# Attention with scaled-and-summed value blocks: halving the pieces of a finished tile's end, and where they are put

## The chip, the cores and the metric

The kernel runs on one core of one Trainium2 chip. The metric is the device time of one launch in microseconds (us): lower is better. Before the change three runs took 559.68, 562.78 and 559.63 us, median 559.68 us.

## What is computed

```python
xn = layernorm(x)                                  # x: 2048 x 448
q  = (xn @ wq) in 16 heads of 256                  # 8 key/value heads, each for two query heads
p  = softmax(q @ k.T / 16)                         # the last 512 cached keys
s  = concat(p @ v) @ wo                            # 2048 x 448
g  = silu((gelu(xn @ w_gate) * (xn @ w_up)) @ w_down)
out = x + s * g
```

The kernel multiplies each value head by its rows of `wo` once, before the attention, so that `p @ (v @ wo)` is added straight into the output sums of a tile, over all 16 heads.

## The kernel before, in words

The first 165 us or so compute the layernorm, the feed-forward part (its gate is written to DRAM) and the products of values and `wo` (`vw`). The rest, which the change touches, is a loop over `NST` = 128 steps (L1045 on): 8 chunks (`c`) of 256 rows times 16 heads (`h`). A chunk is two output tiles of 128 rows. Step n does four things, each in program order on its engine:

- TensorE (PE) makes the scores of step n (`s_jobs`, from `kT` and `qT`, into a ring of three PSUM banks 4 to 6), the queries of step n+2 (`q_jobs`, bank 7), and the product of probabilities and `vw` of step m = n-4 (`pv_jobs`). Every matmul uses 64 of the 128 rows of the array; `halves` (L796) takes two lists, one for the lower and one for the upper 64 rows, and lays them out in one order so that the two halves run side by side. Two matmuls of different halves that add into the same PSUM bank must not overlap: where the half changes on a bank, `halves` makes the second one wait for the end of the first.
- VectorE (DVE) takes a reciprocal of the row sums of step n-1 (`rd`, L863), the row minima of the step's two score tiles (`mn`, L852), and four sums of blocks of the transposed probabilities (`sS`, L888, called `sums`) of step n-3, which PE reads in step n+1.
- ScalarE (ACT) empties the queries (`qT`, L378) and takes the two exponentials (`p`, L857), each of which frees a score bank.
- GpSimd (POOL) multiplies by the reciprocal (the normalizing, `pn`, L873, two tiles a step); a DMA issued by SP then transposes it into `pT`.

The product uses seven block products instead of eight, a fast matrix multiplication over 2 x 2 blocks: products 1 to 7, of which 5, 6, 7 and 3 read `sS`. They are added over the 16 heads in banks 0 to 3 (`AT`, L891): bank 0 holds products 1 and 2, bank 1 products 6 and 7, bank 2 products 4 and 5, bank 3 product 3. `B0` to `B3` are the lists of matmuls of each bank, 4, 4, 4 and 2. `pv_plan` (L915) gives the order in which a head's lists are issued: `one` and `two` to one half, `all_` to the other.

When head 15 of a chunk has been added (a step with `ends`, n = 19, 35, 51, ..., 115), banks 0 to 3 must be emptied into `aS` (seven blocks of 128 x 224, f32) before the next chunk's first head may write them: `evac` (L941), bank 0 and bank 1 by DVE, 2 and 3 by ACT. `finish` (L949) then returns nine pieces that add up the blocks on POOL, multiply by the gate on DVE (`fin`, L964, 128 x 448) and add x on POOL (`add`, L974, 128 x 448); one piece is popped per step (L1106), at the end of the step's program, and the result is stored by a DMA on SP. Each POOL piece has `after=last_sum`: it waits for the last of DVE's four sums of that step. POOL works in order, so the normalizing of the next step stands behind it.

After step 127 a tail adds up the last chunk.

Of the kernel before, what the change touches and what calls it, by code (L numbers as in the profile page):

```python
# [6 lines left out]
ALU = mybir.AluOpType  # L7
# [159 lines left out]
def bass_recurrent_scan__sliding_block_cached__geglu_ffn__prompt_kernel(  # L167
# [36 lines left out]
    with es:  # L204
# [14 lines left out]
        def sbuf_bufs(at, size, n):  # L219
            return [K.buf(at + i * size, size) for i in range(n)]  # L220
# [66 lines left out]
        aS, a, at = place("aS", [P, 7, HN], F32, at=tl)  # L287
        b_aS = sbuf_bufs(a, HN * 4, 7)
        tmp, a, at = place("tmp", [P, 2, D], F32, at=at)
        b_tmp = sbuf_bufs(a, D * 4, 2)  # L290
        NXR = 4
        ofin, a, at = place("ofin", [P, 2, D], BF16, at=at)
        b_ofin = sbuf_bufs(a, D * 2, 2)
        xr, a, at = place("xr", [P, NXR, D], BF16, at=at)
        b_xr = sbuf_bufs(a, D * 2, NXR)
        gr, a, at = place("gr", [P, NXR, D], BF16, at=at)
# [74 lines left out]
        def dma(q, o, i, reads=(), writes=()):  # L371
            K.op(q, lambda e, o=o, i=i: e.dma_start(o, i), reads, writes, dma=True)
# [4 lines left out]
        def act(o, i, func, reads, writes, scale=1.0):  # L377
            K.op("act", lambda e, o=o, i=i: e.activation(o, i, func, scale=scale), reads, writes)  # L378
# [525 lines left out]
        def pv_jobs(n, u, lst, last):  # L904
            h, src = n % Hq, pv_src(n)
            rows = slice(R * u, R * u + R)
            out = []
            for p, j in lst:
                i, s = AT[p]
                a, b = src[p]  # L910
                out.append([i, s * HN, (s + 1) * HN, a[rows, j, :], vw[rows, vslot(h), p - 1, j, :],
                            h == 0 and (u, (p, j)) in FIRST, (u, (p, j)) in last, [b, b_vw[h][p - 1]]])
            return out

        def pv_plan(n):  # L915
            if n % Hq in (0, Hq - 1):
                one, two, all_ = B0 + B2, B3 + B1, B0 + B1 + B2 + B3
            else:
                one, two, all_ = B0 + B2, B1 + B3, B1 + B3 + B2 + B0
            last = LAST if n % Hq == Hq - 1 else TLAST if n == NST - LAG - 1 else ()  # L920
            u = 0 if n + LAG + 2 < NST else 1
            return pv_jobs(n, u, one, last), pv_jobs(n, u, two, last), pv_jobs(n, 1 - u, all_, last)

        def flat(x):
            return [z for y in x for z in y]
# [8 lines left out]
            moves.append(lambda: dma("sp", gr[:, t % NXR, :], gd[t, :, :], (b_gd[t],), (b_gr[t % NXR],)))  # L934

        def store_out(t):
            moves.append(lambda: dma("sp", out_view[:, t, :], ofin[:, t % 2, :], (b_ofin[t % 2],), ()))
            if t + NXR < NT:
                load_fin(t + NXR)

        def evac(i, eng):  # L941
            n = 2 if i < 3 else 1
            o, s = aS[:, 2 * i:2 * i + n, :], bank[i][:, 0:n * HN].rearrange("p (a n) -> p a n", a=n)
            if eng == "act":
                act(o, s, ACT.Copy, (b_ps[i],), b_aS[2 * i:2 * i + n])
            else:
                K.op("dve", lambda e: e.tensor_copy(o, s), (b_ps[i],), b_aS[2 * i:2 * i + n])

        def finish(c, eng):  # L949
            def tt(o, a, b):  # L950
                def go():
                    sl = [aS[:, x[0]:x[-1] + 1, :] for x in (o, a, b)]
                    if len(a) < len(o):
                        sl[1] = sl[1].broadcast_to([P, len(o), HN])
                    K.op(eng, lambda e: e.tensor_tensor(sl[0], sl[1], sl[2], ALU.add),  # L955
                         [b_aS[i] for i in a + b], [b_aS[i] for i in o], after=last_sum)
                return go

            def fin(x):
                def go():  # L960
                    t = 2 * c + x
                    s, y = t % 2, t % NXR
                    sl = slice(1, 7, 5) if x == 0 else slice(4, 6)
                    K.op("dve", lambda e: e.scalar_tensor_tensor(  # L964
                        out=tmp[:, s, :].rearrange("p (a n) -> p a n", a=2), in0=aS[:, sl, :], scalar=sc[:, 1:2],
                        in1=gr[:, y, :].rearrange("p (a n) -> p a n", a=2), op0=ALU.mult, op1=ALU.mult),
                        [b_aS[i] for i in range(7)[sl]] + [b_sc, b_gr[y]], (b_tmp[s],))
                return go

            def add(x):  # L970
                def go():
                    t = 2 * c + x
                    s, y = t % 2, t % NXR
                    K.op(eng, lambda e: e.tensor_tensor(ofin[:, s, :], tmp[:, s, :], xr[:, y, :], ALU.add),  # L974
                         (b_tmp[s], b_xr[y]), (b_ofin[s],), after=last_sum)
                    stores.append(t)
                return go
            return [(eng, tt([1, 2], [0], [1, 2])), (eng, tt([3], [2], [3])), (eng, tt([0], [2], [5])),
                    (eng, tt([4, 5], [3], [4, 5])), ("dve", fin(1)), (eng, add(1)), (eng, tt([6], [0], [6])),
                    ("dve", fin(0)), (eng, add(0))]  # L980


        heads = [*range(3, 13), 2, 13]
        order = []
# [57 lines left out]
            K.reuse(b_gsl[t:t + 1])  # L1042
            act(gsl[:, t, :], gr[:, y, :], ACT.Copy, (b_gr[y], b_sc), (b_gsl[t],), scale=sc[:, 1:2])

        todo, stores, ready, last_sum = [], [], [], []  # L1045
        fill(0)
        for n in range(NST):
            h, m = n % Hq, n - LAG
            c = n // Hq
            more = n + 2 < NST  # L1050
            ends = m >= 0 and m % Hq == Hq - 1
            if n == LAG:
                store_g()
                K.reuse(b_pT[3:] + b_sS[2])
            s0, s1 = s_jobs(n, 0, True), s_jobs(n, 1, not more)
            for t in ready:
                store_out(t)
            ready, stores = stores, []
            if moves and n < NST - 2:
                moves.pop(0)()  # L1060
            if more:
                q0, q1 = q_jobs(n + 2, 0), q_jobs(n + 2, 1)
                q0[1][0][5] = True
                (q1[0] if m >= 0 else q1[1])[-1][6] = True
                if m < 0:
                    q1[0][0][5] = q0[0][-1][6] = True
            if m < 0:
                halves(q1[0] + s0[0] + q0[0] + s1[0], q0[1] + s1[1] + q1[1] + s0[1])
            else:
                one, two, all_ = pv_plan(m)  # L1070
                if more:
                    halves(s0[0] + one + q0[0] + q1[0] + s1[0] + two, q0[1] + q1[1] + s0[1] + s1[1] + all_)
                else:
                    halves(s0[0] + s1[0] + all_, one + s0[1] + s1[1] + two)
            if n >= 1:
                recip(n - 1)
                norm(n - 1)
            row_min(n, 0)
            if more:
                q_evac(n + 2)  # L1080
            if ends:
                evac(0, "dve")
                evac(2, "act")
            row_min(n, 1)
            expo(n, 0)
            expo(n, 1)
            if 3 <= n < NST - 1:
                last_sum = [sums(n - 3, (0, 1, 2, 3))]
            if n < 3:
                fill(n + 1)  # L1090
            if n == 2:
                store_g()
            if n in VW12:
                vw_plain(VW12[n])
            if n in GS:
                gates_scaled(GS[n])
            if n == LAG:
                K.reuse(b_aS + b_tmp + b_ofin + b_xr + b_gr)
                for t in range(NXR):
                    load_fin(t)  # L1100
            if ends:
                evac(1, "dve")
                evac(3, "act")
                todo.extend(finish(m // Hq, "pool"))
            elif todo:
                todo.pop(0)[1]()  # L1106
            if h == LAG and c >= 1 and c + 1 < NC:
                for k in range(NK + 1):
                    moves.append(lambda k=k, y=(c + 1) % 2, d=xnd[c + 1, :, k, :], r=b_xnd[2 * c + 2:2 * c + 4]: dma(
                        "sp", xq[:, y, k, :], d, r, (b_xq[y][k],)))  # L1110
# [57 lines left out]
        for t in range(2):  # L1168
            i, sl = PB[t], (slice(1, 7, 5), slice(4, 6))[t]
            p = two(p32[:, t, 0:D])  # L1170
            add("dve", p, two(bank[i][:, 0:D]), gs[t], [b_ps[i], b_gsl[t]], (b_p32[t],), ALU.mult)
            add(("pool", "dve")[t], two(ofin[:, t, :]), p, aS[:, sl, :], [b_p32[t]] + [b_aS[k] for k in ((1, 6), (4, 5))[t]],
                (b_ofin[t],))
            store_out(NT - 2 + t)
            moves.pop(0)()

# [54 lines left out]
```

## Time and profile before

| what | value |
|---|---|
| median of the three runs | 559.68 us |
| profiled execution: its time / its span | 560.88 us / 559.1 us |
| granted TensorE clock (mean) | 0.999 |
| evacuation, DVE 128 x 448 f32 (L947) | 0.621 us each, 12 after 260 us |
| POOL add of blocks, 128 x 448 / 128 x 224 (L955) | 1.134 / 0.658 us |
| POOL add of x, 128 x 448 (L974) | 1.041 us |
| DVE multiply by the gate, 128 x 448 (L964) | 0.678 us |
| DVE add, one input in PSUM, 128 x 224 (tail, L1114) | 0.380 us |
| POOL normalizing, 128 x 512 (L873) | 0.713 us, two per step |
| DVE sums, 128 x 256 f16 (L888) | 0.282 us median, 0.693 and 0.764 at most |
| matmul of the products, 64 rows x 224 columns | 0.256 us each, several in flight |

The busy time of an engine is the union of its instructions; a matmul's duration includes the time in the pipeline, so two or more overlap. The start of the reciprocal L863 marks the step on DVE; the start of the matmuls with `wqr` marks it on PE.

### The profile page before, as it was taken

To read this page: it belongs to the slowest core of one execution; us is meant where nothing else is said; L and a number is where in the kernel's file an instruction comes from. 1 tells how busy PE (TensorE), PEld (TensorE's weight loads), DVE (VectorE), ACT (ScalarE), POOL (GpSimd) and SP (SyncE) were. 2 spreads that over 40 slices of the span, in tenths; PEclk is the share of its full clock that TensorE was granted. 3 is DMA by queue.
4 is the path that set the end of the run, shared out by engine and by line. 5 is a ranking of instruction groups with operands and counts; after the bars stand their busy time and mean duration, and the time that the engine had idled before them with its cause. 6 is when DMAs were issued, how large, how long until landed. Compare 5 with 4: busy or idle time off the path is not lost.

```text
span 559.1 us, 18710 instructions
## 1 busy us (share of the span) xinstructions
PE 547.2 (98%) x7612; PEld 436.0 (78%) x7612; DVE 462.1 (83%) x1177; ACT 342.1 (61%) x813; POOL 258.9 (46%) x374
## 2 busy tenths in 40 slices
PE   8989999999989999999999999999999999999996
PEld 5644444445546999999999999999999999999983
DVE  6664979857757888998899889889988988988996
ACT  5432323467766676766766676676676666666762
POOL 1121590100004444665476376556546745754665
PEclk9999999999999999999999999999999999999999
DMA  9999999401105865569456666854866675574654
GB/s 263 186 221 156 198 315 200 103 1 30 51 8 98 130 108 93 95 107 136 83 110 126 111 98 108 129 94 89 137 106 96 119 122 93 108 133 92 88 90 96
DMA packets 190245, 66.07 MB, mean 118 GB/s; under 512 B 169408, under 2 KB 187984, under 8 KB 190160
## 3 DMA queue, kind: packets, MB, share of 16 engines
q1 hardware_dynamic: 186928, 56.96, 59.2%
q0 software_dynamic: 2464, 7.34, 4.9%
q8 instruction: 60, 0.98, 0.8%
q10 hardware_dynamic: 768, 0.57, 0.3%
q14 instruction: 25, 0.20, 0.2%
HBM read 19.76 MB, written 5.77 MB: 46 GB/s over the span
## 4 chain that ended last, share of the span: by engine, by line
PE 86%; DVE 8%; DMA 3%; issue 1%; ACT 1%; POOL 0%; SPq 0%; DVEq 0%; ACTq 0%
PE bank L384 85%; DMA pT<-pn 2%; DVE vw L715 1%; DVE vw L726 1%; DVE actT L559 1%; DVE mn L852 1%; DVE sS L888 1%; DMA x<-in_A_x_dram 1%; ACT vw L713 1%; DVE mx L676 1%; ACT gl L378 0%; DVE xn L457 0%; DVE stats L431 0%; DVE g2a L581 0%; POOL rstd L443 0%
## 5 line engine op out<-in xcount | busy, mean ns | idle before, releaser
L384 PE MATMUL bank<-kT,qT 64*128 64x512 bf16 x1024 | 280.0, 376 | 0.0
L873 POOL TENSOR_SCALAR pn<-p,rd 128x512 f16<-128x512 f32 x254 | 177.0, 711 | 178.2 <-DVE rd L863 178.2
L384 PE MATMUL bank<-vw,sS 64*128 64x224 f16 x1984 | 230.2, 256 | 0.8 <-DVE sS L888 0.8
L384 PE MATMUL bank<-xq,wq 64*128 64x256 bf16 x1536 | 218.4, 269 | 0.1
L384 PE MATMUL bank<-vw,pT 64*128 64x224 f16 (+1 forms) x1520 | 208.7, 258 | 1.1 <-DMA pT<-pn 1.1
L852 DVE TENSOR_REDUCE mn<-bank 128x1 f32<-128x512 f32 x256 | 173.4, 684 | 40.2 <-PE bank L384 39.3
L857 ACT ACTIVATE p<-bank,mn 128x512 f32<-128x512 f32 x256 | 175.0, 685 | 9.9 <-DVE mn L852 5.5
L384 PEld LDWEIGHTS bank<-vw,sS 64*128 64x128 f16 x1984 | 161.9, 94 | 11.8 <-DVE sS L888 4.1
L384 PEld LDWEIGHTS bank<-vw,pT 64*128 64x128 f16 (+1 forms) x1520 | 142.5, 94 | 7.4 <-DMA pT<-pn 1.4
L384 PEld LDWEIGHTS bank<-xq,wq 64*128 64x128 bf16 x1536 | 137.9, 94 | 10.4 <-issue 1.9
L378 ACT ACTIVATE qT<-bank 128x512 bf16<-128x512 f32 (+1 forms) x132 | 76.6, 584 | 113.1 <-PE bank L384 112.2
L384 PEld LDWEIGHTS bank<-kT,qT 64*128 64x128 bf16 x1024 | 89.1, 94 | 2.4 <-ACT p L857 1.2
L384 PE MATMUL bank<-xnT,wgu 64*128 64x512 bf16 (+2 forms) x768 | 84.7, 350 | 2.1 <-DVE actT L559 1.7
L888 DVE TENSOR_TENSOR sS<-pT 128x256 f16<-128x256 f16 x248 | 78.8, 357 | 0.4 <-DMA pT<-pn 0.4
L384 PEld LDWEIGHTS bank<-xnT,wgu 64*128 64x128 bf16 x768 | 37.7, 94 | 38.6 <-DVE actT L559 3.0
L384 PE MATMUL bank<-xq,wqr 64*128 64x256 bf16 x256 | 67.5, 269 | 0.0
L378 ACT ACTIVATE gl<-bank 128x512 bf16<-128x512 f32 x56 | 33.1, 597 | 49.7 <-PE bank L384 43.1
L559 DVE TENSOR_TENSOR actT<-bank,gl 128x512 bf16<-128x512 f32 x56 | 37.4, 685 | 16.7 <-PE bank L384 16.0
L857 ACT ACTIVATION_READ_ACCUMULATOR p<-bank,mn 128x1 f32 x256 | 50.6, 198 | 0.0
L384 PE MATMUL bank<-wd,actT 128*128 128x448 bf16 x224 | 45.4, 353 | 0.6 <-DVE actT L559 0.5
L955 POOL TENSOR_TENSOR aS<-aS 128x224 f32<-128x224 f32 (+1 forms) x35 | 29.7, 849 | 30.5 <-DVE rd L863 30.5
L888 DVE TENSOR_TENSOR sS<-sS,pT 128x256 f16<-128x256 f16 x124 | 43.4, 350 | 0.0
(82 smaller groups left out, 412.6 us busy)
## 6 DMA issues: line engine op xcount, KB each, us to landing
wq<-in_A_wq_dram POOLq DMA_DIRECT2D x8, 384.0 KB, 8.8
woa<-in_A_wo_dram POOLq DMA_DIRECT2D x6, 448.0 KB, 6.3
pT<-pn SPq DMA_TRANSPOSE x129, 3.1
xn_t<-xnT SPq DMA_DIRECT2D x16, 128.0 KB, 4.0
xr<-in_A_x_dram SPq DMA_DIRECT2D x16, 112.0 KB, 2.8
gr<-gate_t SPq DMA_DIRECT2D x16, 112.0 KB, 2.9
out_dram<-ofin SPq DMA_DIRECT2D x16, 112.0 KB, 2.0
wd<-in_B_w_down_dram SPq DMA_DIRECT2D x1, 1568.0 KB, 8.7
```

The source lines that it names most:

```text
L378: K.op("act", lambda e, o=o, i=i: e.activation(o, i, func, scale=scale), reads, writes)
L384: ins = e.matmul(o, lhsT=l, rhs=r, start=st, stop=sp)
L559: K.op("dve", lambda e: e.tensor_tensor(actT[c % 2][:, f, :], bank[b + 1], gl[:, s, :], ALU.mult), (b_ps[b + 1], b_gl[s]), (b_actT[c % 2][ ...
L676: K.op("dve", lambda e: e.tensor_reduce(mx[:, i:i + 1], o, AX.XY, ALU.max, apply_absolute_value=True), (b,), (b_mx,))
L713: K.op("act", lambda e: e.activation(v[:, 0, jj, :], o[:, 0:HN], ACT.Copy, scale=sc[:, 0:1]), (b, b_sc), (b_vw[h][0],))
L715: K.op("dve", lambda e: e.scalar_tensor_tensor(out=v[:, 4, jj, :], in0=o[:, HN:D], scalar=sc[:, 0:1], in1=v[:, 0, jj, :], op0=ALU.mult, op ...
L726: K.op("dve", lambda e, o=o, a=a, b=b: e.tensor_tensor(v[:, o, :, :], v[:, a, :, :], v[:, b, :, :], ALU.subtract), (b_vw[h][a], b_vw[h][b] ...
L852: K.op("dve", lambda e: e.tensor_reduce(mn[:, m:m + 1], bank[i], AX.X, ALU.min), (b_ps[i],), (b_mn[m],))
L857: K.op("act", lambda e: e.activation(p32[:, z, :], bank[i], ACT.Exp, bias=mn[:, m:m + 1], scale=-1.0, accum_out=rsum[:, 2 * r + t:2 * r + ...
L873: K.op(engs[t], lambda e, o=o, i=i, s=s: e.tensor_scalar(o, i, s, 1.0, op0=ALU.mult, op1=ALU.mult), (b_p32[z], b_rd[r]), (b_pn[y][t],))
L888: o = K.op("dve", lambda e, i=i, a=a, b=b, f=f: e.tensor_tensor(s[i], a, b, f), r, (b_sS[y][i],))
L955: K.op(eng, lambda e: e.tensor_tensor(sl[0], sl[1], sl[2], ALU.add), [b_aS[i] for i in a + b], [b_aS[i] for i in o], after=last_sum)
```

## The change

Six edits go together.

1. The finished tile's pieces are halved for all chunks but the last that goes through `finish` (c = NC - 2): 13 pieces of 224 columns, in a new order. For c = NC - 2 eight pieces stay unhalved. The dependency records of `tmp` and `ofin` are halved too.
2. `after=last_sum` is gone: a POOL piece no longer waits for DVE's sums and comes directly behind the normalizing of its step.
3. Bank 1 is not copied but added while it is read: two DVE additions of 224 columns write `aS` 2 and 3; the POOL additions that made these two blocks are gone.
4. In a step with `ends` the emptying of bank 1 stands before the fourth of DVE's sums, not behind it.
5. In a chunk's last head one matmul of bank 1 moves into `one`, and bank 3's two go before the second score tile (`mid`).
6. In a chunk's first head the half with `all_` takes bank 1 between the two pairs of bank 0.

```diff
         def pv_plan(n):
-            if n % Hq in (0, Hq - 1):
-                one, two, all_ = B0 + B2, B3 + B1, B0 + B1 + B2 + B3
+            if n % Hq == Hq - 1:
+                one, mid, two, all_ = B0 + B2 + B1[:1], B3, B1[1:], B0 + B1 + B2 + B3
+            elif n % Hq == 0:
+                one, mid, two, all_ = B0 + B2, (), B3 + B1, B0[:2] + B1 + B0[2:] + B2 + B3
             else:
-                one, two, all_ = B0 + B2, B1 + B3, B1 + B3 + B2 + B0
+                one, mid, two, all_ = B0 + B2, (), B1 + B3, B1 + B3 + B2 + B0
...
         def evac(i, eng):
...
+            elif i == 1:
+                for k in range(2):
+                    K.op("dve", lambda e, k=k: e.tensor_tensor(
+                        aS[:, 2 + k, :], bank[1][:, k * HN:(k + 1) * HN], aS[:, 2 * k, :], ALU.add),
+                        (b_ps[1], b_aS[2 * k]), (b_aS[2 + k],))
...
         def finish(c, eng):
...
-                         [b_aS[i] for i in a + b], [b_aS[i] for i in o], after=last_sum)
+                         [b_aS[i] for i in a + b], [b_aS[i] for i in o])
...
-            return [(eng, tt([1, 2], [0], [1, 2])), (eng, tt([3], [2], [3])), (eng, tt([0], [2], [5])),
-                    (eng, tt([4, 5], [3], [4, 5])), ("dve", fin(1)), (eng, add(1)), (eng, tt([6], [0], [6])),
-                    ("dve", fin(0)), (eng, add(0))]
+            a1, a0, a6 = tt([1], [0], [1]), tt([0], [2], [5]), tt([6], [0], [6])
+            if c == NC - 2:
+                z = (0, 1)
+                return [a1, a0, tt([4, 5], [3], [4, 5]), fin(1, z), a6, add(1, z), fin(0, z), add(0, z)]
+            u, v = (0,), (1,)
+            return [a1, a0, tt([4], [3], [4]), fin(1, u), tt([5], [3], [5]), fin(1, v), add(1, u), fin(0, u), a6,
+                    add(1, v), fin(0, v), add(0, u), add(0, v)]
...
-                    halves(s0[0] + one + q0[0] + q1[0] + s1[0] + two, q0[1] + q1[1] + s0[1] + s1[1] + all_)
+                    halves(s0[0] + one + q0[0] + q1[0] + mid + s1[0] + two, q0[1] + q1[1] + s0[1] + s1[1] + all_)
...
-                last_sum = [sums(n - 3, (0, 1, 2, 3))]
+                sums(n - 3, (0, 1, 2))
+                if ends:
+                    evac(1, "dve")
+                sums(n - 3, (3,))
...
             if ends:
-                evac(1, "dve")
                 evac(3, "act")
                 todo.extend(finish(m // Hq, "pool"))
             elif todo:
-                todo.pop(0)[1]()
+                todo.pop(0)()
```

`fin` and `add` take a second argument, the halves `ks` that they work on; `add` hands the tile to the store when its second half is done.

More of the change, by code (lines that the diff above doesn't have):

```diff
@@ L289, in bass_recurrent_scan__sliding_block_cached__geglu_ffn__prompt_kernel @@
         tmp, a, at = place("tmp", [P, 2, D], F32, at=at)
-        b_tmp = sbuf_bufs(a, D * 4, 2)
+        b_tmp = [sbuf_bufs(a + i * D * 4, HN * 4, 2) for i in range(2)]
         NXR = 4
         ofin, a, at = place("ofin", [P, 2, D], BF16, at=at)
-        b_ofin = sbuf_bufs(a, D * 2, 2)
+        b_ofin = [sbuf_bufs(a + i * D * 2, HN * 2, 2) for i in range(2)]
         xr, a, at = place("xr", [P, NXR, D], BF16, at=at)
@@ L915, in pv_plan @@
         def pv_plan(n):
-            if n % Hq in (0, Hq - 1):
-                one, two, all_ = B0 + B2, B3 + B1, B0 + B1 + B2 + B3
+            if n % Hq == Hq - 1:
+                one, mid, two, all_ = B0 + B2 + B1[:1], B3, B1[1:], B0 + B1 + B2 + B3
+            elif n % Hq == 0:
+                one, mid, two, all_ = B0 + B2, (), B3 + B1, B0[:2] + B1 + B0[2:] + B2 + B3
             else:
-                one, two, all_ = B0 + B2, B1 + B3, B1 + B3 + B2 + B0
+                one, mid, two, all_ = B0 + B2, (), B1 + B3, B1 + B3 + B2 + B0
             last = LAST if n % Hq == Hq - 1 else TLAST if n == NST - LAG - 1 else ()
             u = 0 if n + LAG + 2 < NST else 1
-            return pv_jobs(n, u, one, last), pv_jobs(n, u, two, last), pv_jobs(n, 1 - u, all_, last)
+            return [pv_jobs(n, u, x, last) for x in (one, mid, two)] + [pv_jobs(n, 1 - u, all_, last)]
         def flat(x):
@@ L936, in store_out @@
         def store_out(t):
-            moves.append(lambda: dma("sp", out_view[:, t, :], ofin[:, t % 2, :], (b_ofin[t % 2],), ()))
+            moves.append(lambda: dma("sp", out_view[:, t, :], ofin[:, t % 2, :], b_ofin[t % 2], ()))
             if t + NXR < NT:
@@ L955, in go, with fin @@
                     K.op(eng, lambda e: e.tensor_tensor(sl[0], sl[1], sl[2], ALU.add),
-                         [b_aS[i] for i in a + b], [b_aS[i] for i in o], after=last_sum)
+                         [b_aS[i] for i in a + b], [b_aS[i] for i in o])
                 return go
-            def fin(x):
+            def fin(x, ks):
                 def go():
@@ L962, in go, with add @@
                     s, y = t % 2, t % NXR
-                    sl = slice(1, 7, 5) if x == 0 else slice(4, 6)
+                    ids = [((1, 6), (4, 5))[x][k] for k in ks]
+                    sl = slice(ids[0], ids[-1] + 1, max(ids[-1] - ids[0], 1))
+                    two = lambda z: z.rearrange("p (a n) -> p a n", a=2)[:, ks[0]:ks[-1] + 1, :]
                     K.op("dve", lambda e: e.scalar_tensor_tensor(
-                        out=tmp[:, s, :].rearrange("p (a n) -> p a n", a=2), in0=aS[:, sl, :], scalar=sc[:, 1:2],
-                        in1=gr[:, y, :].rearrange("p (a n) -> p a n", a=2), op0=ALU.mult, op1=ALU.mult),
-                        [b_aS[i] for i in range(7)[sl]] + [b_sc, b_gr[y]], (b_tmp[s],))
+                        out=two(tmp[:, s, :]), in0=aS[:, sl, :], scalar=sc[:, 1:2],
+                        in1=two(gr[:, y, :]), op0=ALU.mult, op1=ALU.mult),
+                        [b_aS[i] for i in ids] + [b_sc, b_gr[y]], [b_tmp[s][k] for k in ks])
                 return go
-            def add(x):
+            def add(x, ks):
                 def go():
@@ L973, in go @@
                     s, y = t % 2, t % NXR
-                    K.op(eng, lambda e: e.tensor_tensor(ofin[:, s, :], tmp[:, s, :], xr[:, y, :], ALU.add),
-                         (b_tmp[s], b_xr[y]), (b_ofin[s],), after=last_sum)
-                    stores.append(t)
-                return go
-            return [(eng, tt([1, 2], [0], [1, 2])), (eng, tt([3], [2], [3])), (eng, tt([0], [2], [5])),
-                    (eng, tt([4, 5], [3], [4, 5])), ("dve", fin(1)), (eng, add(1)), (eng, tt([6], [0], [6])),
-                    ("dve", fin(0)), (eng, add(0))]
+                    sl = slice(ks[0] * HN, (ks[-1] + 1) * HN)
+                    K.op(eng, lambda e: e.tensor_tensor(ofin[:, s, sl], tmp[:, s, sl], xr[:, y, sl], ALU.add),
+                         [b_tmp[s][k] for k in ks] + [b_xr[y]], [b_ofin[s][k] for k in ks])
+                    if ks[-1] == 1:
+                        stores.append(t)
+                return go
+            a1, a0, a6 = tt([1], [0], [1]), tt([0], [2], [5]), tt([6], [0], [6])
[5 more added lines that the diff above has]
+                    add(1, v), fin(0, v), add(0, u), add(0, v)]
         heads = [*range(3, 13), 2, 13]
@@ L1043, in gates_scaled @@
             act(gsl[:, t, :], gr[:, y, :], ACT.Copy, (b_gr[y], b_sc), (b_gsl[t],), scale=sc[:, 1:2])
-        todo, stores, ready, last_sum = [], [], [], []
+        todo, stores, ready = [], [], []
         fill(0)
@@ L1069, in bass_recurrent_scan__sliding_block_cached__geglu_ffn__prompt_kernel @@
             else:
-                one, two, all_ = pv_plan(m)
+                one, mid, two, all_ = pv_plan(m)
                 if more:
-                    halves(s0[0] + one + q0[0] + q1[0] + s1[0] + two, q0[1] + q1[1] + s0[1] + s1[1] + all_)
+                    halves(s0[0] + one + q0[0] + q1[0] + mid + s1[0] + two, q0[1] + q1[1] + s0[1] + s1[1] + all_)
                 else:
@@ L1097, in bass_recurrent_scan__sliding_block_cached__geglu_ffn__prompt_kernel @@
             if n == LAG:
-                K.reuse(b_aS + b_tmp + b_ofin + b_xr + b_gr)
+                K.reuse(b_aS + flat(b_tmp) + flat(b_ofin) + b_xr + b_gr)
                 for t in range(NXR):
@@ L1172, in bass_recurrent_scan__sliding_block_cached__geglu_ffn__prompt_kernel @@
             add(("pool", "dve")[t], two(ofin[:, t, :]), p, aS[:, sl, :], [b_p32[t]] + [b_aS[k] for k in ((1, 6), (4, 5))[t]],
-                (b_ofin[t],))
+                b_ofin[t])
             store_out(NT - 2 + t)
```

## The prediction

> **What bounds the kernel now.** I read the page first (busy time and the chain that ended last), then the start of each step's reciprocal in the timeline of VectorE (DVE), then TensorE's (PE's) waits, its weight loads around a chunk's end, and last DVE beside GpSimd (POOL). From the page:
>
> ```profile
> PE 547.2 (98%) x7612; PEld 436.0 (78%) x7612; DVE 462.1 (83%) x1177; ACT 342.1 (61%) x813; POOL 258.9 (46%) x374
> PE 86%; DVE 8%; DMA 3%; issue 1%; ACT 1%; POOL 0%; SPq 0%; DVEq 0%; ACTq 0%
> ```
>
> PE is the bound: whatever DVE and POOL save counts only where PE waits for it. How much PE waits in the regular part (262 to 535 us) is in the waits of its weight loads (us in total, times, longest):
>
> ```profile
> PEld bank L384 <- PE bank L384: 1.8, 11, 0.2
> PEld bank L384 <- DVE sS L888: 1.6, 6, 0.3
> PEld bank L384 <- ACT p L857: 1.1, 6, 0.2
> ```
>
> That is 4.5 us, and it falls at the same places in each chunk (weight loads in time; in brackets the idle time before and what ended it):
>
> ```profile
> 319.21 0.31 PEld L384 LDWEIGHTS bank<-vw,sS 64*128 64x128 f16 x8 [0.16 <-PE bank L384]
> ...
> 320.88 0.09 PEld L384 LDWEIGHTS bank<-kT,qT 64*128 64x128 bf16 x1 [0.17 <-ACT p L857]
> ...
> 322.36 0.31 PEld L384 LDWEIGHTS bank<-vw,sS 64*128 64x128 f16 x8 [0.16 <-PE bank L384]
> ...
> 338.84 0.09 PEld L384 LDWEIGHTS bank<-vw,sS 64*128 64x128 f16 x1 [0.27 <-DVE sS L888]
> ```
>
> What they cost is read from DVE's reciprocals, one per step:
>
> ```profile
> 273.52 0.17 DVE L863 RECIPROCAL rd<-rsum 128x2 f32<-128x2 f32 x1
> ...
> 316.79 0.48 DVE L888 TENSOR_TENSOR sS<-pT 128x256 f16<-128x256 f16 x2
> ...
> 321.53 0.17 DVE L863 RECIPROCAL rd<-rsum 128x2 f32<-128x2 f32 x1
> ...
> 328.98 0.89 DVE L888 TENSOR_TENSOR sS<-pT 128x256 f16<-128x256 f16 x2
> ```
>
> From 273.52 to 321.53 lie 16 steps: 48.01 us. An undisturbed step takes 2.97 (308.86, 311.83, 314.80), so 16 would take 47.52, and a chunk loses 0.50. On PE itself (first `wqr` matmul of each step) the loss is placed: 317.11 to 320.26 is 3.15 (0.18 lost, the last head's step with the wait at 319.21), 320.26 to 323.41 again 3.15 (0.18, the first head's step with 320.88 and 322.36; one of the two is hidden, since only 0.18 shows), 338.26 to 344.34 is 6.08 for two (0.14, the wait for the sums). **Seven chunk ends times 0.50 are 3.5 us: more than this the regular part can't give back.**
>
> **The change, part by part,** per chunk end, the two matmul orders first.
>
> Last head. Before, the lower half's first matmul of bank 1 comes four matmuls behind the upper half's last one there; those in the lower half are two of 224 columns, at 0.095 us from one to the next (316.99, 317.08, 317.18), 0.19 in all, and 0.16 is waited. In an ordinary head the same pair has a 512-column score matmul between (0.21 from start to start: 317.22, 317.43) and no wait. The gap needed is thus about 0.19 + 0.16 = 0.35. After the change, the lower half has a score matmul and the upper one three of 224 columns between (0.21 and 0.29, after what is left of the matmul before): 0.29 to 0.38. Left: 0 to 0.06. I take -0.15; ends 0 (another wait takes its place) and -0.18.
>
> First head. The bank 1 pair gets eight places apart, with two more 224-column matmuls between, which is enough. But bank 3 then stands bare: the upper half's first matmul there follows the lower half's last by three 224-column matmuls, 0.29 against 0.35 needed; before, that lay behind the wait on bank 1. So about 0.06 to 0.10 of the 0.16 stays, and the exponential's wait of 0.17 remains, because bank 2 is still emptied by ACT before that exponential. I take -0.05; ends 0 and -0.18.
>
> Bank 1 while it is emptied. One copy of 0.62 becomes two additions; the second reads what the first writes, so 0.38 + 0.05 + 0.38 = 0.81, or +0.19 on DVE, where the tail's row for an addition from PSUM has 0.38. It now stands before the fourth sum (0.29), so bank 1 is free some 0.1 earlier. But the first head's upper half also wants it two matmuls earlier. No PE wait names the copy today, so nothing is gained by it; the cover is the time between DVE's 321.44 and PE's first bank 1 matmul about 321.7. I take +0.03; ends 0 and +0.19 (all of the extra time reaches PE). The fourth sum is read last of the four by PE, so its delay costs nothing.
>
> Pieces halved, and behind the normalizing. This is the doubtful part. POOL and DVE get in each other's way: a pair of sums takes 0.48 alone (316.79 above), 0.89 where a normalizing runs (328.98 above):
>
> ```profile
> 327.54 0.66 POOL L955 TENSOR_TENSOR aS<-aS 128x224 f32<-128x224 f32 x1 [0.95 <-DVE rd L863]
> 328.17 1.36 POOL L873 TENSOR_SCALAR pn<-p,rd 128x512 f16<-128x512 f32 x2
> ...
> 333.44 1.14 POOL L955 TENSOR_TENSOR aS<-aS 128x448 f32<-128x448 f32 x1 [0.95 <-DVE rd L863]
> 334.54 1.51 POOL L873 TENSOR_SCALAR pn<-p,rd 128x512 f16<-128x512 f32 x2
> ```
>
> Before, a piece waits for the sums and pushes the next normalizing back, so that this one meets the sums. A 448-column piece lengthens DVE's step by about 0.45 (the step to 327.37 takes 3.42, those with 224 columns 2.95), a 448-column `fin` the one to 337.03 to 3.76, and by 338.84 PE waits 0.27. Afterwards the normalizing starts 0.25 behind the reciprocal and ends 1.6 behind it; the piece (0.66) runs from 1.6 to 2.26, and DVE's first sum falls due at about 2.0 (314.80 to 316.79). So it meets 0.26 of a piece, not a normalizing of 0.7, and `fin` lengthens a step by about 0.38, with 0.5 of idle DVE time in each. The wait at 338.84 should go: -0.14 (ends 0 and -0.14). In its place nine POOL pieces per chunk can hold up the first sum. The cover is the time until PE reads it: in an ordinary step it ends at 316.79 + 0.28 = 317.07 and PE's first matmul with it starts at 317.56, weights loaded 0.09 earlier: 0.40. The pairs of 0.89 and more (0.41 late, three steps running after 325.95) show that such lateness costs PE nothing. I take +0.05 per chunk; ends 0 and, if POOL's next instruction overtakes a sum that waits, 0.66 - 0.40 = 0.26 at each of nine pieces, 2.3 per chunk. Against the second speaks 334.54: there a sum that had waited got in between the two normalizings (1.51 instead of 1.36 for the pair). That is why I stay near the lower end.
>
> The Trainium skill's page "SBUF — State Buffer", section "Who interferes with whom", speaks against this edit: a VectorE instruction with two SBUF inputs and a GpSimd instruction that reads SBUF exclude each other for the whole instruction. The rows differ a little: the first sum at 328.98 starts at about 329.39, 0.14 before the recorded end of the normalizing (329.53). By the rule at its word, 0.14 more at nine pieces and seven ends, uncovered, would add an estimated 8.8 us; by the rows nothing beyond the 0.05 above. The same section lets the additions of bank 1 go free, with one SBUF input; no run here shows it yet.
>
> SP: a tile's store and its two reloads are issued four steps later, one per step as before, each 0.58 on the queue between transposes 2.97 apart. Four buffers, hence two chunks, cover it: 0.
>
> Last `finish` (eight pieces, unhalved): the second `fin` (0.68) comes a step earlier, out of step 123, whose DVE work is on the chain from 535.5 on; but `tt` of 448 (1.14) and `add` (1.04) now stand behind the normalizing, where they can hold the sums 0.6 longer. Once: -0.2, ends -0.59 (the chain's share of `fin`) and +0.6.
>
> The sum: -0.15 - 0.05 + 0.03 - 0.14 + 0.05 = -0.26 per chunk end; times 7 = -1.8; with the tail -2.0. The profiled execution would go from 560.88 to 558.9. It lies 1.2 above the median of the runs shown; the difference carries over: **559.68 - 2.0 = 557.7 us.**
>
> **The rivals.**
>
> Waits only change places (chance 0.27): PE's orders gain 0.15, but DVE, loaded by 0.19 more in the same step, or the exponential's bank sends PE into another wait. For it: of 0.33 waited in the first head's step only 0.18 shows, so one wait already hides another. Against: DVE idles 0.2 to 0.6 per step. Then 7 x (0 to 0.1) saved: 559 to 559.7.
>
> All of it goes (0.12): 7 x 0.50 and the tail's 0.59: 559.68 - 4.1 = 555.6. Against: bank 3 in the first head.
>
> Slower (0.10): POOL's piece takes its turn in front of a waiting sum. It decides from the point where the first sum is over 0.40 late; then up to 0.26 x 9 x 7 = 16 us: 576; if only one piece in four does it, 4 us: 563.7. Against: 334.54.
>
> The orders don't do what they say: that is the bank 3 pair, in the main sum already.
>
> **How the numbers follow.** Main forecast 0.51: 556.5 to 558.8. About 1% (5.6 us) is what a measurement of this kernel can tell from no change. Faster by more than that would need more than all the waits listed (4.1): 0.03, for what I don't see. Slower by more: the larger part of the slower rival, 0.06. The rest, 0.91, lies within. The range goes from all waits gone (555.6, rounded down to 555.5) to nothing gained with some loss: 559.7 + 7 x (0.19 + 0.05) for bank 1 and the sums + 0.6 for the tail = 562.0.
>
> **What would show it.** In the profile after: no wait of a weight load at the last head's bank 1; a shorter one, on bank 3, in the first head; none on `sS` five steps later; 16 steps in about 47.75. Pairs of sums near 0.6 rather than 0.9 in the steps with pieces. If instead many weight loads wait for `sS`, or steps with pieces exceed 2.97 on PE, the piece behind the normalizing was the mistake; if the period stays at 48.0 with other names in the brackets, the waits have only moved.

## The result, and the profile after

The changed kernel takes 556.68 us (median of 7, 556.61 to 559.01) against 560.02 us of the kernel before in the same comparison: ratio 0.994, interval 0.9919 to 0.9961. Timed again later beside another set of runs it was 556.49 against 559.30 us, ratio 0.9953 (0.9939 to 0.9967). So it saves about 2.8 to 3.3 us, half a percent, where 2.0 were forecast. The time lies inside the range, and at the lower edge of the main forecast (556.5 to 558.8).

The page after, busy time and the chain that ended last:

```profile
PE 544.7 (98%) x7612; PEld 437.6 (79%) x7612; DVE 465.5 (84%) x1196; ACT 341.3 (62%) x813; POOL 250.3 (45%) x385
PE 86%; DVE 9%; DMA 2%; issue 1%; ACT 1%; POOL 0%; SPq 0%; DVEq 0%; ACTq 0%
```

PE is still the bound, with as many matmuls. DVE is busier by 3.4 us, POOL less by 8.6, and neither decides. What has changed is what PE waits for. Waits of the weight loads between 262 and 535 us (idle times up to 0.15 us are not in this list):

```profile
PEld bank L384 <- DVE sS L888: 1.1, 3, 0.4
PEld bank L384 <- ACT p L857: 1.1, 6, 0.2
```

The waits of PE for itself (1.8 us, 11 times) are gone, and so are the waits for the sums in the chunks with halved pieces. The three that remain all lie behind 516 us, each behind one of the three POOL pieces of 448 columns that the last chunk still has (the last of them, an addition of x, is shown first):

```profile
532.63 1.07 POOL L984 TENSOR_TENSOR ofin<-tmp,xr 128x448 bf16<-128x448 f32 x1
...
518.75 0.09 PEld L384 LDWEIGHTS bank<-vw,sS 64*128 64x128 f16 x1 [0.40 <-DVE sS L888]
...
527.86 0.09 PEld L384 LDWEIGHTS bank<-vw,sS 64*128 64x128 f16 x1 [0.30 <-DVE sS L888]
...
534.10 0.09 PEld L384 LDWEIGHTS bank<-vw,sS 64*128 64x128 f16 x1 [0.41 <-DVE sS L888]
```

The exponential's wait remains, once per chunk. Less than a microsecond behind it the weight loads stop once more, from 318.96 to 319.09 (0.13 us, again once per chunk), until DVE's additions of bank 1 have ended at 319.04:

```profile
318.41 0.09 PEld L384 LDWEIGHTS bank<-kT,qT 64*128 64x128 bf16 x1 [0.17 <-ACT p L857]
...
318.86 0.09 PEld L384 LDWEIGHTS bank<-xq,wq 64*128 64x128 bf16 x1
319.09 0.09 PEld L384 LDWEIGHTS bank<-vw,sS 64*128 64x128 f16 x1
```

DVE's reciprocals, 16 steps apart, give the length of a chunk, and beside them stand the additions of bank 1, a pair of sums and the reciprocal behind it:

```profile
271.49 0.16 DVE L863 RECIPROCAL rd<-rsum 128x2 f32<-128x2 f32 x1
...
318.23 0.81 DVE L950 TENSOR_TENSOR aS<-bank,aS 128x224 f32<-128x224 f32 x2
...
319.15 0.16 DVE L863 RECIPROCAL rd<-rsum 128x2 f32<-128x2 f32 x1
...
320.45 1.12 DVE L888 TENSOR_TENSOR sS<-pT 128x256 f16<-128x256 f16 x2
```

319.15 - 271.49 = 47.66 us, against 48.01 before and 47.52 for 16 undisturbed steps: of the 0.50 lost per chunk 0.35 is back and 0.15 remains. PE's first `wqr` matmul of each step tells where:

```profile
314.82 0.27 PE L384 MATMUL bank<-xq,wqr 64*128 64x256 bf16 x1
...
317.79 0.27 PE L384 MATMUL bank<-xq,wqr 64*128 64x256 bf16 x1
...
320.92 0.27 PE L384 MATMUL bank<-xq,wqr 64*128 64x256 bf16 x1
```

The last head's step takes 2.97 (3.15 before), so it loses nothing. The first head's takes 3.13 (3.15 before): there the remaining 0.16 is lost, with the exponential's wait and the one for bank 1 in it. Most of it is the exponential's: in experiment 4, where the same order meets bank 1 without any idle time, the step still takes 3.10.

The pair of sums at 320.45 takes 1.12 us, longer than any before (0.97), and PE is only just not held up by it: the third sum ends at 321.78, and the weight load that reads it starts at 321.83.

Where the time came from, by stretches of the two first profiles and of one more profile of each kernel (us, from one reciprocal to another):

| stretch | before | before, again | after | after, again |
|---|---|---|---|---|
| start to step 4 | 177.14 | 175.90 | 175.85 | 175.63 |
| steps 4 to 20 | 48.01 | 48.01 | 47.96 | 47.97 |
| steps 20 to 36 | 48.37 | 48.09 | 47.68 | 47.66 |
| steps 36 to 116 (5 chunks) | 240.09 | 240.13 | 238.34 | 238.30 |
| steps 116 to 128 | 34.92 | 34.91 | 34.51 | 34.48 |
| step 128 to the end | 10.57 | 10.66 | 10.56 | 10.46 |
| span | 559.1 | 557.7 | 554.9 | 554.5 |

The first two spans lie 4.2 us apart, the second two 3.2. Of the second: six chunks 48.09 + 240.13 - 47.66 - 238.30 = 2.26, the last steps 0.43, the rest 0.5 in stretches where little or nothing differs.

### The profile page after: what moved, and what is told of

The parts are those of the page before. It is cut to its first block, busy times and chain, and to the rows that moved or that the text cites. A ratio compares the mean times of both kernels' runs of the same rounds, so it can differ in the third digit from the quotient of the medians.

```text
span 554.9 us, 18732 instructions
## 1 busy us (share of the span) xinstructions
PE 544.7 (98%) x7612; PEld 437.6 (79%) x7612; DVE 465.5 (84%) x1196; ACT 341.3 (62%) x813; POOL 250.3 (45%) x385
## 4 chain that ended last, share of the span: by engine, by line
PE 86%; DVE 9%; DMA 2%; issue 1%; ACT 1%; POOL 0%; SPq 0%; DVEq 0%; ACTq 0%
PE bank L384 86%; DVE mn L852 1%; DVE sS L888 1%; DVE vw L715 1%; DVE vw L726 1%; DVE actT L559 1%; DMA x<-in_A_x_dram 1%; DMA pT<-pn 1%; ACT vw L713 1%; DVE mx L676 1%; DVE xn L457 0%; DVE stats L431 0%; ACT gl L378 0%; DVE g2a L581 0%; POOL rstd L443 0%
## 5 line engine op out<-in xcount | busy, mean ns | idle before, releaser
L873 POOL TENSOR_SCALAR pn<-p,rd 128x512 f16<-128x512 f32 x254 | 173.1, 695 | 227.6 <-DVE rd L863 227.6
L384 PE MATMUL bank<-vw,sS 64*128 64x224 f16 x1984 | 222.3, 256 | 0.8 <-DVE sS L888 0.5
L384 PEld LDWEIGHTS bank<-xq,wq 64*128 64x128 bf16 x1536 | 139.6, 94 | 9.4 <-issue 1.9
L384 PEld LDWEIGHTS bank<-kT,qT 64*128 64x128 bf16 x1024 | 93.5, 94 | 2.1 <-ACT p L857 1.2
L888 DVE TENSOR_TENSOR sS<-pT 128x256 f16<-128x256 f16 x248 | 89.8, 402 | 0.0
L888 DVE TENSOR_TENSOR sS<-pT,sS 128x256 f16<-128x256 f16 x124 | 36.1, 291 | 4.0
L384 PEld LDWEIGHTS bank<-wd,actT 128*128 128x128 bf16 x224 | 21.3, 98 | 22.7 <-issue 1.7
```

The source lines that it names most:

```text
L384: ins = e.matmul(o, lhsT=l, rhs=r, start=st, stop=sp)
L873: K.op(engs[t], lambda e, o=o, i=i, s=s: e.tensor_scalar(o, i, s, 1.0, op0=ALU.mult, op1=ALU.mult), (b_p32[z], b_rd[r]), (b_pn[y][t],))
L888: o = K.op("dve", lambda e, i=i, a=a, b=b, f=f: e.tensor_tensor(s[i], a, b, f), r, (b_sS[y][i],))
```

## The experiments

All start from the kernel after, except the first and the tenth. The ratio is to the kernel before, timed in the same comparison, with its 95% interval in brackets; a chunk's length is the distance of DVE's reciprocals 16 steps apart, the same within 0.03 us from step 36 on unless two values are given.

**1. The matmul orders alone**, in the kernel before: parts 5 and 6 of the change (`pv_plan`, and `mid` in the call of `halves`), and nothing else.

> The kernel before with the new matmul orders alone (last and first head); pieces, waits and the copy of bank 1 as before. A chunk of 16 steps takes 48.02 us before and 47.67 after the change. Theory A, the waits add up: the two waits on bank 1 (0.16 each, 0.36 of the 0.50 lost with the exponential's) go, the wait for the sums (0.14) stays; the chunk takes 47.81 and the whole about 1.5 us less than before. Rival B, the waits change places: PE comes earlier to sums that VectorE has not made earlier, so the wait for the sums grows from 0.27 to about 0.4 or a second one appears; the chunk takes 47.95 to 48.02.

It takes 559.48 us, ratio 1.0003 (0.9990 to 1.0017): nothing is gained; the chunk takes 48.00. The rival's numbers are right, with another wait than it named. The waits of weight loads over five chunks (262 to 505 us):

```profile
PEld bank L384 <- DVE aS L949: 1.3, 5, 0.3
PEld bank L384 <- DVE sS L888: 1.3, 5, 0.3
PEld bank L384 <- ACT p L857: 0.9, 5, 0.2
PEld bank L384 <- PE bank L384: 0.8, 4, 0.2
```

PE waits less for itself (0.8 instead of 1.5), but once per chunk 0.27 for the copy of bank 1 (L949): the first head's new order takes that bank two matmuls of its half earlier, and the copy is not done. PE's first head's step takes 3.26 here (3.13 after) and its last head's 3.10 (2.97 after).

**2. The old orders**, the rest as after.

```diff
-                one, mid, two, all_ = B0 + B2 + B1[:1], B3, B1[1:], B0 + B1 + B2 + B3
+                one, mid, two, all_ = B0 + B2, (), B3 + B1, B0 + B1 + B2 + B3
-                one, mid, two, all_ = B0 + B2, (), B3 + B1, B0[:2] + B1 + B0[2:] + B2 + B3
+                one, mid, two, all_ = B0 + B2, (), B3 + B1, B0 + B1 + B2 + B3
```

> The kernel after with the old matmul orders in the first and the last head; the rest of the change kept. Theory A, the waits add up: both waits of 0.16 on bank 1 come back, the wait for the sums stays gone; the chunk takes 47.88 (47.67 + 0.21). Rival B: the pieces and the sums alone carry the gain and the orders were hidden behind the exponential's wait; the chunk takes 47.67 to 47.72.

It takes 558.41 us, ratio 0.9972 (0.9961 to 0.9984); a chunk takes 47.88, as theory A has it. Two waits of 0.16 per chunk are back, and also a wait for the sums of 0.18 (at 327.78), which theory A expected to stay away. With the rest of the change in place, the orders are thus worth 0.21 per chunk; without it (1) 0.02.

**3 and 4. One of the two orders each** (the first or the second pair of lines of 2 undone).

> The kernel after with the first head's old order; the last head's new order kept. My prediction's step (bank 3 stands bare in the first head's new order, little is gained there): one wait of 0.16 on bank 1 comes back in the first head and the chunk takes 47.72 (0.05 more than after). Rival: the whole 0.18 of that step comes back, 47.85. Third: the wait returns but is hidden, because only 0.18 of 0.33 us waited in that step showed before: 47.67.

> The kernel after with the last head's old order; the first head's new order kept. Prediction's step: the last head's wait of 0.16 comes back and costs 0.15, the chunk takes 47.82. Rival: it is hidden by the exponential's wait that follows (0.17 in the profile after), because PE then reaches the score bank later: the chunk takes 47.67 and the exponential's wait is shorter.

With the first head's old order 557.06 us (0.9957, 0.9941 to 0.9972), chunk 47.72, one of six at 47.82. That is the prediction's 0.05, but by luck: 0.02 of it is the first head's step (3.15 instead of 3.13), and 0.03 the last head's (3.00 instead of 2.97), whose order wasn't touched. With the last head's old order 557.88 us (0.9969, 0.9955 to 0.9983), and the chunk takes 47.81 and 47.69 in turn: 0.14 and 0.02. Neither answer to the fourth is right alone. How far the lower half runs behind the upper one differs from chunk to chunk there, and with it what the same order costs (last section). The two singles add up to 0.07 to 0.19, both together are 0.21.

**5. The pieces wait for the sums again**, in all chunks.

```diff
-                         [b_aS[i] for i in a + b], [b_aS[i] for i in o])
+                         [b_aS[i] for i in a + b], [b_aS[i] for i in o], after=last_sum)
-                sums(n - 3, (3,))
+                last_sum = [sums(n - 3, (3,))]
```

(and the same `after` in `add`)

> The kernel after, but GpSimd's pieces wait for the last of VectorE's four sums again, as before the change (all chunks). Theory A, the place behind the normalizing matters: the next normalizing is pushed back, the pairs of sums take 0.9 in every step with a piece, and a wait for the sums comes back; the chunk takes 47.75 to 47.81 (47.67 after). Rival B, halving alone is enough: with pieces of 0.66 VectorE's step in the profile before took 2.95, under PE's 2.97, so no wait comes back and the chunk takes 47.67. In the last chunk, whose pieces are whole, waiting keeps 1.1 us pieces off the sums: the waits of 0.40 and 0.30 at 518.75 and 527.86 should go under B.

It takes 556.14 us, ratio 0.9936 (0.9913 to 0.9959); a chunk takes 47.66, and the stretch from step 116 to 128 34.06 instead of 34.51. The rival is right: no wait for the sums over 0.1 us comes back in the halved chunks, so with halved pieces the place behind the normalizing gains nothing. Whole pieces that wait, with the rest of the change kept in all chunks, were not tried. GpSimd's timeline with a piece that waits:

```profile
324.39 0.66 POOL L962 TENSOR_TENSOR aS<-aS 128x224 f32<-128x224 f32 x1 [0.95 <-DVE rd L863]
325.02 1.35 POOL L873 TENSOR_SCALAR pn<-p,rd 128x512 f16<-128x512 f32 x2
```

and DVE's, the pair of sums beside that normalizing:

```profile
326.12 0.59 DVE L888 TENSOR_TENSOR sS<-pT 128x256 f16<-128x256 f16 x2
```

A piece of 0.66 pushes the normalizing to where it meets the sums with its end only: 0.59, not the 0.95 of the same step after the change. DVE is busy with sums for 16.1 us over a chunk this way and for 19.7 behind the normalizing; the chunk's length is the same.

**6. Whole pieces in all chunks**, behind the normalizing.

```diff
-            if c == NC - 2:
+            if c < NC:
```

> The kernel after with whole pieces (eight, 448 columns where they had 448) in all chunks, behind the normalizing. Theory: the last chunk of the profile after shows what a whole piece does there, waits of 0.40 and 0.30 behind the 1.1 us addition of two blocks and the 1.0 us addition of x; with a second addition of x that is 0.7 to 1.0 per chunk, so a chunk takes 48.4 to 48.7 and the whole is slower than before (by 1 to 4 us). Rival: the sums get in between and it costs under 0.2, the chunk takes 47.7 to 47.9.

It takes 561.24 us, ratio 1.0034 (1.0020 to 1.0047): slower than before, as expected; a chunk takes 48.45, 0.78 more than after, with three waits for the sums (0.40, 0.30, 0.40), one behind each whole piece. GpSimd's timeline with the addition of two blocks:

```profile
328.02 1.36 POOL L873 TENSOR_SCALAR pn<-p,rd 128x512 f16<-128x512 f32 x2 [0.85 <-DVE rd L863]
329.35 1.19 POOL L962 TENSOR_TENSOR aS<-aS 128x448 f32<-128x448 f32 x1
```

DVE's timeline, the sums beside it:

```profile
329.26 1.42 DVE L888 TENSOR_TENSOR sS<-pT 128x256 f16<-128x256 f16 x2
330.61 0.28 DVE L888 TENSOR_TENSOR sS<-sS,pT 128x256 f16<-128x256 f16 x1
```

and the weight load of PE that waited:

```profile
330.94 0.09 PEld L384 LDWEIGHTS bank<-vw,sS 64*128 64x128 f16 x1 [0.40 <-DVE sS L888]
```

The pair ends behind the piece, and PE goes on 0.05 after the end of the third sum (330.89), not of the first. In the program the first sum feeds product 5, in `one`; the third feeds product 6, with which the ordinary `all_` begins.

**7. Bank 1 copied at its old place**, and added up on GpSimd.

```diff
-            elif i == 1:
+            elif i == 9:
...
-                if ends:
-                    evac(1, "dve")
                 sums(n - 3, (3,))
...
             if ends:
+                evac(1, "dve")
                 evac(3, "act")
...
-            return [a1, a0, tt([4], [3], [4]), fin(1, u), tt([5], [3], [5]), fin(1, v), add(1, u), fin(0, u), a6,
+            return [a1, a3, a0, tt([4], [3], [4]), fin(1, u), tt([5], [3], [5]), fin(1, v), add(1, u), fin(0, u), a6,
```

(`a1` = `tt([1, 2], [0], [1, 2])` whole, `a3` = `tt([3], [2], [3])`; one piece more in the last chunk too)

> The kernel after, but bank 1 is copied (0.62 us on VectorE) behind the fourth sum and added up on GpSimd, as before; pieces halved otherwise (14, with the first a whole one of 448 columns). Theory A, the adding while emptying is worth nothing by itself (taken at +0.03 in the prediction, a loss): the chunk takes 47.64 to 47.70. Rival B: the whole first piece (1.1 us) behind the normalizing, right after the chunk's end when VectorE is latest, holds the sums and brings a wait for them of 0.2 to 0.4: 47.85 to 48.0.

It takes 561.20 us, ratio 1.0028 (1.0017 to 1.0039); a chunk takes 48.09 to 48.21. That is more than either theory has: the wait for the sums that B expected (0.40, behind the whole first piece), and the wait for bank 1 of experiment 1, which none expected. The weight loads there:

```profile
320.60 0.09 PEld L384 LDWEIGHTS bank<-vw,sS 64*128 64x128 f16 x1 [0.27 <-DVE aS L954]
...
323.64 0.09 PEld L384 LDWEIGHTS bank<-vw,sS 64*128 64x128 f16 x1 [0.40 <-DVE sS L888]
```

The last chunk takes 35.84, 1.3 more than after; how much of it is the additional piece was not tried.

**9. The additions of bank 1 behind the fourth sum.**

```diff
+                sums(n - 3, (3,))
                 if ends:
                     evac(1, "dve")
-                sums(n - 3, (3,))
```

> The kernel after with bank 1's two additions behind the fourth sum instead of before it. After the change PE's first matmul of bank 1 starts 0.06 behind the end of the additions (319.10 and 319.04), so PE takes the bank the moment it is free. Theory A: the place carries the gain; the additions end 0.2 to 0.3 later, PE waits for them in the first head (0.25 to 0.35) and the chunk takes 47.9 to 48.0 (47.67 after). Rival B: the adding itself (two pieces fewer on GpSimd) carries it and the fourth sum's 0.2 is hidden: under 47.75.

It takes 560.15 us, ratio 1.0016 (1.0006 to 1.0026); a chunk takes 48.16 to 48.19 (one 47.99), more than theory A has. DVE's timeline:

```profile
319.33 0.81 DVE L950 TENSOR_TENSOR aS<-bank,aS 128x224 f32<-128x224 f32 x2
```

and PE's weight load that waits for them:

```profile
320.19 0.09 PEld L384 LDWEIGHTS bank<-vw,sS 64*128 64x128 f16 x1 [0.46 <-DVE aS L950]
```

The additions end at 320.14 and PE goes on 0.05 later, having waited 0.46. Two lines in another order are worth 0.51 per chunk, all that the change gains and more. Not all of it is this wait: PE's first head's step takes 3.46 (3.13 after), but its last head's also takes 3.10 (2.97 after), since smaller waits for the sums (0.18 and 0.15) come with it. In the one chunk of 47.99 the last head's step is 2.97. A copy of bank 1 at the early place was not tried, so the additions are not told from a copy there.

**8 and 11. The last chunk's pieces wait for the sums**, the others don't (5's `after` with `if c == NC - 2`).

> The kernel after; in the last chunk that goes through the pieces (unhalved there) GpSimd's pieces wait for the sums again. If the two waits of 0.40 and 0.30 for the sums in that chunk come from the whole pieces behind the normalizing, they go and the end comes 0.3 to 0.7 us earlier than after. Rival: VectorE's tail from 530 us on sets the end, and nothing is gained (within 0.1).

> The kernel after with the last chunk's pieces waiting for the sums, timed again beside the kernel after. From the profiles 0.5 us less (34.03 against 34.51 from step 116 to 128), so 0.1% under the kernel after; the intervals will hardly part.

It takes 556.19 us (0.9935, 0.9913 to 0.9958), and in the second measurement 556.22 (0.9948, 0.9935 to 0.9960). From step 116 to 128 it takes 34.03 and 34.06, against 34.51 and 34.48: 0.4 to 0.5 less, and the three waits of 0.40, 0.30 and 0.41 are gone (one of 0.18 has come in). With 5, whose 556.14 is not told from it, this is the best version found. The times beside the kernel after (556.22 and 556.49) agree, but their intervals overlap; that it beats the kernel after is shown by the traces alone.

**10 and 12. The two kernels once more.**

> The kernel before once more, for a second profile. Two pieces of the difference between the two profiles are in doubt: the start up to step 4 (177.14 before, 175.85 after, with the same program there) and the second chunk (48.37 against 48.02 in the others, with a wait of 0.55 and 0.20 for a transposing DMA). If they are a matter of the one execution, this profile has a start of 175.5 to 176.5 and a second chunk of 48.02 to 48.15; if they belong to the kernel before, 177 and 48.3 or more.

> The kernel after, timed again on the chip that the run before uses: 0.994 of the kernel before, 0.5 us above the run with the last chunk's pieces waiting; its chunk of 16 steps 47.67 again.

The answers are in the table of stretches. Start and second chunk of the first profile of before (177.14 and 48.37) were a matter of that execution: they are 175.90 and 48.09 here. The kernel after has 0.9953 and a chunk of 47.66.

## Why the prediction was right, and where its steps were off

On PE's steps, which the prediction used to place the loss, its terms per chunk come out like this:

| term | predicted | measured |
|---|---|---|
| last head | -0.15 | -0.18 (3.15 to 2.97) |
| first head, with bank 1 | -0.05 + 0.03 | -0.02 (3.15 to 3.13) |
| wait for the sums | -0.14 | -0.14 (6.08 to 5.94 for the two steps) |
| behind the normalizing | +0.05 | 0.00 to +0.01 (5) |

- **What bounds the kernel** held: the 0.50 that PE lost per chunk was the whole stock, and the gain came out of it.
- **Last and first head**: undoing both costs 0.21 (2), and the bank 3 pair of the first head, which I feared, shows no wait in the profile after. But the prediction gave each order a fixed price, and the experiments show that there is none: the last head's new order costs between 0.00 and 0.13, the old one between 0.06 and 0.19, according to the distance between the two halves (last section). At equal distance the new order gains 0.05 to 0.06. That the step came out near -0.15 is partly luck. The first head's order gives its 0.05 where bank 1 is free in time (4: 3.10 against 3.15 before), but what remains there is the exponential's wait and not the bank 3 pair, so this size was right for a wrong reason.
- **Bank 1 while it is emptied** is the step whose reasoning failed. "No PE wait names the copy today, so nothing is gained by it" was argued with the order of before, where PE comes to bank 1 at about 321.7 and the copy ends at 321.44. The new order comes earlier: after the change PE starts there 0.06 behind the additions (319.10 and 319.04). As a loss, +0.03 was about right (3.13 against the 3.10 of experiment 4). What it missed is that the early place is a condition of the gain: without it the chunk is slower than before (9, 0.51 more than after). I had moved two steps and priced each against the old position of the other. That the sum was still near is luck: both are in the change.
- **Halving** was taken at -0.14 for the wait for the sums: it is gone, also without the new place (5). With whole pieces behind the normalizing the chunk loses 0.78 (6).
- **Behind the normalizing**, taken at +0.05, costs 0.00 to 0.01 per chunk (47.67 and 47.66) and 0.45 once in the last chunk; it gains nothing anywhere. The reasoning was off in two places. The first sum was to fall due about 2.0 us behind the reciprocal and to meet only the end of a piece, with pairs near 0.6; right behind a chunk's end it falls due after 1.30 (319.15 to 320.45), the pair meets the whole piece and takes 0.95 to 1.12. And the cover was reasoned on the wrong sum: I measured how late the first sum may be (0.40), but it is the second that is held:

```profile
320.45 0.45 DVE L888 TENSOR_TENSOR sS<-pT 128x256 f16<-128x256 f16 x1
320.83 0.75 DVE L888 TENSOR_TENSOR sS<-pT 128x256 f16<-128x256 f16 x1
...
320.74 0.69 POOL L962 TENSOR_TENSOR aS<-aS 128x224 f32<-128x224 f32 x1
```

  The first sum waited for the normalizing, which ends at 320.77, and was done at 320.91; the second ended only behind the piece. So a sum that waits got in between two POOL instructions here, and PE reads the second and third sum later. With a piece of 1.2 us even that isn't enough (6).
- **Last chunk**: for the stretch from step 116 on the prediction has -0.26 - 0.2 = -0.46, and it is -0.41 and -0.43, by another way than forecast. `fin` still lies on the chain that ended last (0.59, at 530.53), and up to step 125 nothing is gained (27.42 us from step 116 before, 27.46 after), since the three waits for the sums came in. The gain is the step from 125 to 126, 3.15 before and 2.70 after: before, the ninth piece (POOL, 540.90) pushes the normalizing back there and a sum beside it takes 0.69 (542.94); after the change there is no ninth piece. Waiting pieces save about 0.45 more (8).
- **Sum**: -0.26 x 7 - 0.2 against -0.35 to -0.38 x 6 and -0.43 (and -0.04 in steps 4 to 20). The size was off because the loss of +0.05 did not arrive and the last head gave 0.03 more.

The Trainium skill's page "SBUF — State Buffer", section "Who interferes with whom", has a VectorE instruction with two SBUF inputs and a GpSimd instruction that reads SBUF exclude each other, and the lengthened sums agree (0.45 and 0.75 instead of 0.28 for the pair at 320.45). Taken at its word for every piece, the prediction's estimate of 8.8 us, it would have made the change a loss; what decides is which sum is held, and for that the trace was needed. The same section lets a VectorE instruction with one SBUF input go free. The additions of bank 1 can't show it, since no GpSimd instruction runs beside them (0.388 us on average); the three of the same shape in the tail, from 545.09 on, run beside GpSimd instructions that read SBUF and take 0.380, which agrees.

## What to carry to other kernels

Two edits that meet at one buffer have one price: where an order makes an engine come earlier, ask when the buffer is free in the new order, not in the old one. Where two engines hold each other up, as VectorE and GpSimd did here, ask how long one piece is before asking where it stands: halved pieces cost nothing in either place, whole ones 0.78 per chunk behind the normalizing. What counts is which of the held instructions the bound engine needs first. And the time that the bound engine loses against its undisturbed steps is an upper limit that costs one look.

## What was not expected of the hardware

The order of matmuls on the two halves of the array has no fixed price. With the last head's old order (4) chunks of the same program take 47.69 and 47.81 in turn, over all six chunks. What differs is the distance between the halves, here the time from the upper half's `wqr` matmul of a step to the lower half's. In undisturbed steps around 310 us it is 0.97 us before and 0.84 after, at the same 2.97 us per step. Before:

```profile
314.14 0.27 PE L384 MATMUL bank<-xq,wqr 64*128 64x256 bf16 x1
315.11 0.27 PE L384 MATMUL bank<-xq,wqr 64*128 64x256 bf16 x1
```

After:

```profile
311.85 0.27 PE L384 MATMUL bank<-xq,wqr 64*128 64x256 bf16 x1
312.69 0.27 PE L384 MATMUL bank<-xq,wqr 64*128 64x256 bf16 x1
```

Over six chunks of all fourteen profiles the distance in the step before the last head goes with what that head's step takes (us, undisturbed 2.97):

| distance | last head's step, old order | new order |
|---|---|---|
| 0.83 to 0.85 | 3.03 | 2.97 to 2.98 |
| 0.86 to 0.89 | 3.04 | 2.98 to 3.02 |
| 0.92 to 0.95 | 3.10 to 3.13 | 3.05 |
| 0.97 | 3.15 to 3.16 | 3.10 |

The first head brings the distance to 0.83 (new order) or 0.87 (old order), and a wait of the lower half for the sums then raises it. In experiment 4 this explains the turns:

```profile
328.07 0.09 PEld L384 LDWEIGHTS bank<-vw,sS 64*128 64x128 f16 x1 [0.18 <-DVE sS L888]
```

Such a wait is there in every other chunk, behind a last head at 0.84. The upper half's steps stay at 2.97, so it seems to cost nothing, but the distance goes from 0.83 to 0.94, and the next last head takes 3.12 to 3.13 instead of 3.03. The odd chunks of 3 (47.82) and 9 (47.99) fit as well. So a wait that looks hidden can be paid for later in the chunk. No run set the distance by itself, so this is read from the traces and not tested.
